# Retention and MLP on one core: folding decay into the query casts, evacuating attention by ACT, and issuing crossbar transposes from SP

## The chip, the cores and the metric

The kernel runs on one core of one Trainium2 chip. The metric is device time in microseconds (us) of one execution; a kernel is executed several times, and medians and ranges are given. Profiles show one execution each, so a profile's span is close to the median but need not equal it.

In the profile, PE is the matmul engine and PEld its weight loads, DVE the vector engine, ACT the scalar engine, POOL the GpSimd engine, and SP the engine that only issues DMAs. A name such as SPq or ACTq means the instruction queue of that engine, when it issues DMAs.

## The reference

Eight batches of eight heads, sequence 576, head dimension 64. Attention is a causal retention: scores are scaled by 1/8 and multiplied by a decay gamma to the power of the distance. The result feeds an MLP whose activation is h * cos(h).

```python
scores = scale * q @ k.T
ret    = scores * where(i >= j, gamma[h] ** (i - j), 0)
x      = (ret @ v)            # reordered to [4608 tokens, 512]
h      = x @ w_in             # 512 -> 2048
out    = (h * cos(h)) @ w_out # 2048 -> 512
```

## The kernel before

The sequence is cut into 40 chunks of 128 positions (the last of each batch has 64). For each chunk the kernel loads K, Q and V in float32, casts them to bf16, transposes K and Q, computes scores inside the chunk, adds the contribution of a running state, and writes the result `XT` for the MLP. The MLP works on nine blocks of 512 tokens: `mlp1` (four matmuls, a cosine on ACT, a product on DVE) sixteen times, then `mlp2` (sixteen matmuls for each of four output tiles, evacuated by ACT into `os`). Attention for a later block is interleaved with the MLP pieces of the current ones.

In this program every engine has its own list of instructions and waits at each until what it needs is ready. A DMA is issued by an instruction in one engine's list, so the issue waits its turn there and holds up whatever follows (a timeline below shows a cosine held up for 3.76 us in this way). The parts that matter:

```python
# decay on the output side: one multiply per chunk on DVE (UP is a table of gamma^i / 8)
def ev_o(g, ob, key):   DVE: XT = ob * UP                 # 128x512
def ev_st(g):           DVE: two copies 64x256, state ST -> SBD
def ev_s(g):            DVE: PT = SC * TRI                # 128x1024
def cast_q(d, engs):    POOL: two plain casts 128x512     # K: a cast; V: a multiply by gamma^-j

# transposes for chunk >= 10, by DMA through the crossbar, in ACT's queue
def move_k(g):          ACT: dma_start_transpose(KT <- NAT)    # waits until POOL has cast
def move_q(d):          ACT: dma_start_transpose(QT <- QNAT)
# (chunks 0..9: transposed by PE, most copied out of PSUM by ACT)

def step(g):            # one unit of attention work
    mm_inter(g); mm_st(g); mm_intra(g); mm_s(g + 1)        # PE
    ev_o(g); ev_st(g); ev_s(g + 1)                         # DVE, back to back

BYPE, LEAD = 10, 2
def T(g):               # called before step(g - 1)
    if g < BYPE: transposes of chunk g by PE
    x = g + LEAD
    if x >= BYPE: move_q(x), move_k(x)
    load_to(g + LEAD + 4); cast_to(g + LEAD + 2)
```

The attention score, state and output matmuls write PSUM; the MLP and the attention outputs share a rotation of five PSUM banks, one or two of them held by `mlp2`. The program lets a bank be written again only after its readers on ACT and DVE are done.

## Time and profile before

| | before |
|---|---|
| median, range (first three executions) | 347.7 us, 345.6 to 349.9 |
| profiled span | 346.2 us |
| PE busy | 89% |
| DVE, ACT, POOL busy | 56%, 41%, 28% |

The first two parts of the profile page of the kernel before: busy time per engine, and the span in 40 slices of 8.7 us (a digit is the busy share in tenths; PEclk is the granted PE clock in tenths; in the DMA row, a digit is the mean busy share of the DMA engines).

```profile
PE 307.4 (89%) x2337; PEld 158.8 (46%) x2374; DVE 194.1 (56%) x335; ACT 141.6 (41%) x233; POOL 96.2 (28%) x138
PE   6489998676779987999999989999998999999997
ACT  6727533435324433433343334443434333444421
PEclk9879999968789999999999999999999999999999
DMA  9999898999944996496747993666742101100012
```

PE looks nearly full, but an average hides stages. In slices 7 to 12 (52 to 104 us) PE is at 6 to 8 tenths, its clock falls, and DMA is saturated until about 95 us. After that PE is near full, and DMA is in most slices not.

To measure stages I use landmarks that every run has: the moments at which ACT begins to evacuate the output tiles `os`. There are 37 of them; the fourth ends block 0, the fifth is the first of block 1. Before, these are at 42.2 us (first), 57.3 (fourth), 107.6 (fifth) and 343.8 (last). Between the fourth and fifth lie all of `mlp1` of block 1 and the first pieces of block 2.

The view of waits of the kernel before (who waited for what: total us, number of times, longest) names the releasers (a selection).

```profile
PEld bk L444 <- DVE xt L399: 9.4, 10, 1.8
PEld bk L466 <- ACT os L481: 9.0, 13, 2.1
PE bk L444 <- DVE gt L454: 8.0, 5, 2.6
PE bk L444 <- DVE xt L399: 7.5, 8, 1.8
ACT cb L451 <- POOL nat L228: 6.0, 2, 3.8
PE bk L466 <- ACT os L481: 4.2, 4, 1.6
```

The fifth line is odd at first sight: a cosine (`cb`) reads nothing that POOL writes. The timeline of ACT between 61 and 67 us shows why it waited. Lines hold start, duration, engine, source line, operation, operands and, in brackets, the idle time before.

```profile
61.96 0.59 ACT L226 ACTIVATE kt<-bk 128x512 bf16<-128x512 bf16 x1
63.21 1.33 ACTq L302 DMA_TRANSPOSE qt<-qnat  x1
64.57 1.69 ACTq L296 DMA_TRANSPOSE kt<-nat  x1
66.30 0.95 ACT L451 ACTIVATE cb<-bk,cpi 128x320 bf16<-128x320 f32 x2 [3.76 <-POOL nat L228]
```

The transpose of Q stands in ACT's queue and waits for POOL's cast, which waits for a load. Then two issues take 1.33 and 1.69 us. Only then can ACT compute the cosines; DVE's products wait for these, and PE for DVE's (`gt`, the third line of the waits).

### The profile page before, as it was taken

The numbers are of one execution on the slowest core, as the hardware profiler recorded it, in microseconds if no ns is written. First come the engines' busy times: TensorE is split into PE (matmuls) and PEld (weight loads), VectorE is DVE, ScalarE is ACT, GpSimd is POOL, SyncE is SP. The second block draws the span as 40 slices with busy tenths as digits, with TensorE's granted clock in tenths as the row PEclk, the third lists the DMA queues.
The fourth block names the chain that finished last, engine by engine and source line by source line (L and its number), as shares of the span: only waits on it lengthen the run. The fifth ranks groups of instructions, "written<-read, shape, count | busy, mean of one in ns | idle before, by whom it ended". The sixth has DMA issues, their size and how long they took to land.

```text
span 346.2 us, 6065 instructions
## 1 busy us (share of the span) xinstructions
PE 307.4 (89%) x2337; PEld 158.8 (46%) x2374; DVE 194.1 (56%) x335; ACT 141.6 (41%) x233; POOL 96.2 (28%) x138
## 2 busy tenths in 40 slices
PE   6489998676779987999999989999998999999997
PEld 2355454444645434444454444444444444444444
DVE  3677524566764766556675756565764666433300
ACT  6727533435324433433343334443434333444421
POOL 3560357446413341331331531422330000000000
PEclk9879999968789999999999999999999999999999
DMA  9999898999944996496747993666742101100012
GB/s 187 234 186 192 197 234 218 213 242 243 214 87 84 213 242 122 103 212 152 148 104 114 249 211 97 157 148 169 136 118 66 47 31 56 38 32 30 30 61 93
DMA packets 133117, 49.43 MB, mean 143 GB/s; under 512 B 105312, under 2 KB 128608, under 8 KB 133088
## 3 DMA queue, kind: packets, MB, share of 16 engines
q1 hardware_dynamic: 99152, 37.76, 49.1%
q10 hardware_dynamic: 29184, 7.08, 13.1%
q0 software_dynamic: 4752, 4.19, 7.8%
q8 instruction: 19, 0.31, 0.4%
q14 instruction: 10, 0.08, 0.1%
HBM read 36.70 MB, written 9.44 MB: 133 GB/s over the span
## 4 chain that ended last, share of the span: by engine, by line
PE 70%; ACT 6%; issue 6%; DVE 4%; POOL 4%; ACTq 3%; DMA 3%; SPq 3%; DVEq 0%; POOLq 0%
PE bk L444 33%; PE bk L466 29%; ACT cb L451 3%; ACTq L296 3%; SPq L198 2%; PE sc L320 2%; POOL nat L238 2%; DVE gt L454 2%; PE st L346 2%; DMA stg<-in_v_dram 2%; PE bk L387 2%; POOL qnat L228 2%; DVE xt L399 1%; PE bk L372 1%; DMA qstg<-in_q_dram 1%
## 5 line engine op out<-in xcount | busy, mean ns | idle before, releaser
L451 ACT ACTIVATE cb<-bk,cpi 128x512 bf16<-128x512 f32 (+3 forms) x164 | 102.6, 635 | 159.4 <-PE bk L444 119.7
L444 PE MATMUL bk<-xt,win 128*128 128x512 bf16 (+3 forms) x634 | 147.3, 363 | 21.0 <-DVE gt L454 8.0
L454 DVE TENSOR_TENSOR gt<-bk,cb 128x512 bf16<-128x512 f32 (+3 forms) x164 | 100.7, 624 | 108.8 <-ACT cb L451 87.0
L466 PE MATMUL bk<-wout,gt 128*128 128x512 bf16 (+1 forms) x578 | 142.7, 374 | 5.5 <-ACT os L481 4.2
L444 PEld LDWEIGHTS bk<-xt,win 128*128 128x128 bf16 x656 | 62.5, 101 | 80.7 <-DVE xt L399 9.4
L466 PEld LDWEIGHTS bk<-wout,gt 128*128 128x128 bf16 x592 | 56.1, 98 | 71.0 <-ACT os L481 9.0
L228 POOL CAST nat<-stg 128x512 bf16<-128x512 f32 (+1 forms) x36 | 21.9, 609 | 127.7 <-PE st L346 80.2
L331 DVE TENSOR_TENSOR pt<-sc,tri 128x1024 bf16<-128x1024 f32 (+1 forms) x40 | 44.6, 1114 | 7.7 <-PE sc L320 6.7
L238 POOL TENSOR_TENSOR nat<-stg,wv 128x512 bf16<-128x512 f32 (+1 forms) x40 | 41.6, 1041 | 18.8 <-DMA stg<-in_v_dram 18.7
L481 ACT ACTIVATE os<-bk 128x512 f32<-128x512 f32 (+1 forms) x37 | 21.7, 585 | 30.2 <-PE bk L466 25.5
L399 DVE TENSOR_TENSOR xt<-bk,up 128x512 bf16<-128x512 f32 (+1 forms) x40 | 26.7, 669 | 11.8 <-PE bk L387 10.9
L228 POOL CAST qnat<-qstg 128x512 bf16<-128x512 f32 (+1 forms) x44 | 25.8, 613 | 13.9 <-DMA qstg<-in_q_dram 13.9
L359 DVE CAST sbd<-st 64x256 bf16<-64x256 f32 x64 | 26.5, 414 | 1.0
L320 PE MATMUL sc<-qt,kt 64*128 64x128 bf16 (+1 forms) x320 | 15.9, 222 | 1.4 <-DVE qt L228 1.2
L387 PE MATMUL bk<-pt,nat 128*64 128x128 bf16 (+1 forms) x320 | 15.8, 223 | 0.5 <-DVE pt L331 0.5
L372 PEld LDWEIGHTS bk<-qt,sbd 128*128 128x128 bf16 x128 | 9.7, 102 | 7.4 <-ACT os L481 1.5
L372 PE MATMUL bk<-qt,sbd 128*128 128x128 bf16 (+1 forms) x128 | 12.0, 218 | 1.0 <-ACT os L481 1.0
L320 PEld LDWEIGHTS sc<-qt,kt 64*128 64x128 bf16 (+1 forms) x320 | 9.3, 100 | 6.1 <-issue 1.7
L387 PEld LDWEIGHTS bk<-pt,nat 128*64 128x64 bf16 (+1 forms) x320 | 10.4, 114 | 1.6 <-DVE pt L331 1.1
L346 PE MATMUL st<-nat 128*64 128x64 bf16 x256 | 10.4, 205 | 0.2 <-POOL nat L238 0.2
L346 PEld LDWEIGHTS st<-nat 128*64 128x64 bf16 x256 | 6.8, 114 | 5.9 <-issue 3.5
L226 ACT ACTIVATE kt<-bk 128x512 bf16<-128x512 bf16 (+1 forms) x10 | 5.5, 550 | 4.6 <-PE bk L266 4.6
(35 smaller groups left out, 46.5 us busy)
## 6 DMA issues: line engine op xcount, KB each, us to landing
out_dram<-os SPq DMA_DIRECT2D x35, 256.0 KB, 2.3
stg<-in_k_dram SPq DMA_DIRECT2D x32, 256.0 KB, 5.0
qstg<-in_q_dram SPq DMA_DIRECT2D x16, 512.0 KB, 5.8
stg<-in_v_dram SPq DMA_DIRECT2D x32, 256.0 KB, 5.8
wout<-in_moe_w_out_dram POOLq DMA_DIRECT2D x4, 512.0 KB, 13.8
win<-in_moe_w_in_dram POOLq DMA_DIRECT2D x3, 512.0 KB, 6.0
stg<-in_k_dram SPq DMA_DIRECT2D x8, 128.0 KB, 3.7
qstg<-in_q_dram SPq DMA_DIRECT2D x8, 128.0 KB, 3.4
```

Source lines behind the costliest of these rows:

```text
L228: self.P.add(eng, lambda e: e.tensor_copy(dst, src), r=r, w=w)
L238: self.P.add(eng, lambda e: e.tensor_tensor(ap(self.NAT[na], 2 * DM, 0, n, DM, [D, H], [1, D]), ap(self.STG[st], 2 * DM, 0, n, DM, [D, H], ...
L320: inst = e.matmul(ap(self.SC, 1024, 0, n, hp * 512 + c * 128, [1, n]), ap(kt, DM, 64 * hp, 64, c * 128, [1, n]), self.queries(g, 64 * hp, ...
L331: self.P.add("dve", lambda e: e.tensor_tensor(ap(pt, 1024, 0, n, 0, [128, 8], [h, 2], [1, h]), ap(self.SC, 1024, 0, n, 0, [128, 8], [h, 2] ...
L359: self.P.add("dve", lambda e, hp=hp: e.tensor_copy(ap(self.SBD[g % self.NSB], 512, 64 * hp, 64, 64 * hp, [128, 4], [1, 64]), ap(self.ST, 5 ...
L372: inst = e.matmul(ap(ob, 512, 0, 128, c * 128, [1, n]), ap(sbd, 512, 0, 128, c * 128, [1, 128]), self.queries(g, 0, 128, c), start=(c == 0 ...
L387: inst = e.matmul(ap(ob, 512, 64 * hp, 64, c * 128, [1, n]), ap(na, 2 * DM, 0, n, DM + (2 * c + hp) * D, [1, D]), ap(pt, 1024, 0, n, hp * ...
L399: self.P.add("dve", lambda e: e.tensor_tensor(ap(self.XT, 4 * TOK, 0, 128, b * S + CH * r, [TOK, 4], [1, 2], [2, h]), ap(ob, 512, 0, 128, ...
L444: inst = e.matmul(ap(ps, 512, 0, 128, 0, [1, n]), ap(self.WIN, 4 * DFF, 0, 128, c * DFF + 128 * f, [1, 128]), ap(self.XT, 4 * TOK, 0, 128, ...
L451: self.P.add("act", lambda e: e.activation(ap(cb, TB, 0, 128, 0, [1, n]), ap(ps, 512, 0, 128, 0, [1, n]), AF.Sin, bias=self.CPI.ap(), scal ...
L454: self.P.add("dve", lambda e: e.tensor_tensor(ap(gt, NF * TB, 0, 128, f * TB + lo - TB * j, [1, n]), ap(ps, 512, 0, 128, 0, [1, n]), ap(cb ...
L466: return e.matmul(ap(ps, 512, 0, 128, 0, [1, cn]), ap(gt, NF * TB, 0, 128, f * TB + 128 * t, [1, 128]), ap(self.WOUT, NF * DM, 0, 128, f * ...
```

## The change

Its intent was to relieve DVE and ACT at once. The decay and the scale are multiplied into Q when it is cast, so the output evacuation becomes a plain copy and can go to ACT, as can the state. The 48 transposes go to SP, which computes nothing, ahead of the next loads, and three chunks early instead of two. The score and state evacuations become separate units, spread between MLP pieces. The early transposes' copies go to DVE (those of K for the first four chunks stay on ACT), and the order of the first four chunks changes. The core of the diff:

```diff
-    self.P.add("act", lambda e: e.dma_start_transpose(   # move_k, move_q
+    self.P.add("sp", lambda e: e.dma_start_transpose(
-    cast_q: copy
+    cast_q: tensor_tensor(..., WT[gamma^i / 8] broadcast, mult)     # POOL (chunks 0..3: DVE and POOL)
-    ev_o: dve tensor_tensor(XT, ob, UP, mult)
+    ev_o: self.copy("act", XT, ob)
-    ev_st: dve tensor_copy x2
+    ev_st: self.copy("act", ...) x2
     def step(self, g):
         ...
         self.ev_o(g, ob, key)
-        self.ev_st(g)
-        if g + 1 < len(CHUNKS):
-            self.ev_s(g + 1)
-        BYPE, LEAD = 10, 2
+        BYPE, LEAD = 10, 3
-                    self.step_tq(dbl(g))
-                self.step_tk(g)
+                    self.step_tq(dbl(g), "dve")
+                self.step_tk(g, "dve")
                 out += [lambda g=g: T(g + 1), lambda g=g: self.step(g)]
+                if g + 1 < NC:
+                    out.append(lambda g=g: self.ev_s(g + 1))
+                out.append(lambda g=g: self.ev_st(g))
[... decay tables UP (ACT, 8 instructions) replaced by a 128x88 table; the head reordered: the first weights
 gated on chunk 1's V instead of chunk 2's K, 8 instead of 4 pieces of mlp1 in halves of 256 columns ...]
```

More of the change, by code (lines that the diff above doesn't have):

```diff
@@ L124, in __init__ @@
         self.OS = [sb(f"os{i}", [128, DM], F32) for i in range(self.NOS)]
-        self.UP = sb("up", [128, 4 * S], F32)
-        self.WV = sb("wv", [128, 40], F32)
+        self.WT = sb("wt", [128, 88], F32)
         self.IDN = sb("idn", [128, 128], BF16)
@@ L130, in __init__ @@
         self.DUM = sb("dum", [128, 512], BF16)
-        self.IG = sb("ig", [128, S], F32)
-        self.IV = sb("iv", [128, 40], F32)
-        self.LV = sb("lv", [128, 40], F32)
-        self.LU = sb("lu", [128, 4], F32)
+        self.IV = sb("iv", [128, 88], F32)
+        self.LV = sb("lv", [128, 88], F32)
         self.CLN = sb("cln", [128, 1], F32)
@@ L154, in constants @@
         lng = [math.log(1.0 - 2.0 ** (-5.0 - h)) for h in range(H)]
-        P.add("pool", lambda e: e.iota(ap(self.IG, S, 0, 128, 0, [1, 512]), [[128, 4], [1, 2], [2, 64]], base=0,
-                                       channel_multiplier=0, allow_small_or_imprecise_dtypes=True), w=["ig0"])
-        P.add("pool", lambda e: e.iota(self.IV.ap(), [[128, 5], [0, 8]], base=0, channel_multiplier=1,
-                                       allow_small_or_imprecise_dtypes=True), w=["iv"])
+        P.add("pool", lambda e: e.iota(ap(self.IV, 88, 0, 128, 0, [1, 40]), [[128, 5], [0, 8]], base=0,
+                                       channel_multiplier=1, allow_small_or_imprecise_dtypes=True), w=["iv0"])
@@ L159, in constants @@
+        P.add("pool", lambda e: e.iota(ap(self.IV, 88, 0, 128, 40, [1, 48]), [[256, 3], [1, 2], [0, 8]], base=0,
+                                       channel_multiplier=2, allow_small_or_imprecise_dtypes=True), w=["iv1"])
         P.add("dve", lambda e: e.memset(self.ONE.ap(), 1.0), w=["one"])
         P.add("dve", lambda e: e.memset(self.DUM.ap(), 0.0), w=["dum"])
+        for h in range(H):
+            P.add("dve", lambda e, h=h: e.memset(ap(self.LV, 88, 0, 128, h, [8, 5]), -lng[h]), w=[("lv", h)])
+            P.add("dve", lambda e, h=h: e.memset(ap(self.LV, 88, 0, 128, 40 + h, [8, 6]), lng[h]), w=[("lv", h + 8)])
@@ L161, in constants @@
         P.add("dve", lambda e: e.memset(self.CLN.ap(), math.log(1.0 / 8.0)), w=["cln"])
-        for h in range(H):
-            P.add("dve", lambda e, h=h: e.memset(ap(self.LU, 4, 64 * (h % 2), 64, h // 2, [1, 1]), lng[h]),
-                  w=[("lu", h)])
-        for h in range(H):
-            P.add("dve", lambda e, h=h: e.memset(ap(self.LV, 40, 0, 128, h, [8, 5]), -lng[h]), w=[("lv", h)])
+        P.add("dve", lambda e: e.memset(self.CPI.ap(), math.pi / 2), w=["cpi"])
         P.add("dve", lambda e: e.tensor_tensor(self.LV.ap(), self.IV.ap(), self.LV.ap(), ALU.mult),
-              r=["iv"] + [("lv", h) for h in range(H)], w=["lvx"])
@@ L169, in constants @@
-        P.add("dve", lambda e: e.memset(self.CPI.ap(), math.pi / 2), w=["cpi"])
+              r=["iv0", "iv1"] + [("lv", h) for h in range(16)], w=["lvx"])
         for i in range(self.NSB):
             P.add("dve", lambda e, i=i: e.memset(self.SBD[i].ap(), 0.0), w=[("sbd", i)])
-        self.decay(0, 256, "ig0")
-        P.add("act", lambda e: e.activation(self.WV.ap(), self.LV.ap(), AF.Exp), r=["lvx"], w=["wv"])
+        P.add("act", lambda e: e.activation(ap(self.WT, 88, 0, 128, 0, [1, 40]), ap(self.LV, 88, 0, 128, 0, [1, 40]),
+                                            AF.Exp), r=["lvx"], w=["wv"])
@@ L174, in constants @@
+        P.add("act", lambda e: e.activation(ap(self.WT, 88, 0, 128, 40, [1, 48]), ap(self.LV, 88, 0, 128, 40, [1, 48]),
+                                            AF.Exp, bias=self.CLN.ap()), r=["lvx", "cln"], w=["wq"])
         P.add("pool", lambda e: e.affine_select(self.IDN.ap(), self.ONE.ap(), pattern=[[1, 128]],
@@ L179, in constants @@
                                                 channel_multiplier=-1), r=["one"], w=["tri"])
-        P.add("pool", lambda e: e.iota(ap(self.IG, S, 0, 128, 512, [1, 64]), [[1, 2], [2, 32]], base=512,
-                                       channel_multiplier=0, allow_small_or_imprecise_dtypes=True), w=["ig1"])
-    def decay(self, lo, hi, *keys):
-        for c in range(4):
-            self.P.add("act", lambda e, c=c: e.activation(
-                ap(self.UP, 4 * S, 0, 128, c * S + lo, [1, hi - lo]), ap(self.IG, S, 0, 128, lo, [1, hi - lo]), AF.Exp,
-                bias=self.CLN.ap(), scale=ap(self.LU, 4, 0, 128, c, [1, 1])),
-                r=list(keys) + ["cln", ("lu", 2 * c), ("lu", 2 * c + 1)], w=[("up", lo, c)])
+        self.sin_table()
     def sin_table(self):
@@ L240, in cast_v @@
             ap(self.STG[st], 2 * DM, 0, n, DM, [D, H], [1, D]),
-            ap(self.WV, 40, 0, n, 8 * r, [1, H], [0, D]), ALU.mult),
+            ap(self.WT, 88, 0, n, 8 * r, [1, H], [0, D]), ALU.mult),
             r=[("stg", st, 1), "wv"], w=[("nat", na, 1)])
@@ L246, in cast_q @@
         for x, eng in enumerate(engs):
-            self.copy(eng, ap(self.QNAT[k], 2 * DM, 0, n, x * DM, [D, H], [1, D]),
-                      ap(self.QSTG[k], 2 * DM, 0, n, x * D, [2 * D, H], [1, D]), [("qstg", k)], [("qnat", k, x)])
+            self.P.add(eng, lambda e, x=x: e.tensor_tensor(
+                ap(self.QNAT[k], 2 * DM, 0, n, x * DM, [D, H], [1, D]),
+                ap(self.QSTG[k], 2 * DM, 0, n, x * D, [2 * D, H], [1, D]),
+                ap(self.WT, 88, 0, n, 40 + 16 * (d % 3) + 8 * x, [1, H], [0, D]), ALU.mult),
+                r=[("qstg", k), "wq"], w=[("qnat", k, x)])
     def bank(self, hold=False):
@@ L301, in move_q @@
         n, k, t = (128, 128, 32)[d % 3], d % self.NQ, d % self.NQT
-        self.P.add("act", lambda e: e.dma_start_transpose(
+        self.P.add("sp", lambda e: e.dma_start_transpose(
             ap(self.QT[t], 2 * DM, 0, 128, 0, [128, 8], [1, n]), ap(self.QNAT[k], 2 * DM, 0, n, 0, [1, 2 * DM])),
@@ L358, in ev_st @@
         for hp in range(2):
-            self.P.add("dve", lambda e, hp=hp: e.tensor_copy(
-                ap(self.SBD[g % self.NSB], 512, 64 * hp, 64, 64 * hp, [128, 4], [1, 64]),
-                ap(self.ST, 512, 64 * hp, 64, 0, [64, 4], [1, 64])),
-                r=["st"], w=[("sbd", g % self.NSB, hp)])
+            self.copy("act", ap(self.SBD[g % self.NSB], 512, 64 * hp, 64, 64 * hp, [128, 4], [1, 64]),
+                      ap(self.ST, 512, 64 * hp, 64, 0, [64, 4], [1, 64]), ["st"], [("sbd", g % self.NSB, hp)])
     def mm_inter(self, g, ob, key):
@@ L398, in ev_o @@
         h = n // 2
-        self.P.add("dve", lambda e: e.tensor_tensor(
-            ap(self.XT, 4 * TOK, 0, 128, b * S + CH * r, [TOK, 4], [1, 2], [2, h]),
-            ap(ob, 512, 0, 128, 0, [128, 4], [h, 2], [1, h]),
-            ap(self.UP, 4 * S, 0, 128, CH * r, [S, 4], [h, 2], [1, h]), ALU.mult),
-            r=[key] + [("up", 0 if r < 2 else 256, c) for c in range(4)], w=[("xt", g)])
+        self.copy("act", ap(self.XT, 4 * TOK, 0, 128, b * S + CH * r, [TOK, 4], [1, 2], [2, h]),
+                  ap(ob, 512, 0, 128, 0, [128, 4], [h, 2], [1, h]), [key], [("xt", g)])
     def step_s(self, g):
@@ L562, in warm @@
             self.P.add("pe", mm, r=["one", "dum"], w=[("bk", 0)])
-        def heads(g):
-            self.cast_k(g, "act")
-            if pair(g):
-                self.cast_q(dbl(g), ("act", "dve"))
-            self.cast_v(g, "pool")
-            self.step_tk(g)
-            if pair(g):
-                self.step_tq(dbl(g), "dve")
+        two = ("dve", "pool")
         load_to(4)
         warm(8)
-        heads(0)
+        self.cast_k(0, "act")
+        self.cast_q(0, two)
+        self.cast_v(0, "pool")
+        self.step_tk(0)
+        self.step_tq(0, "dve")
         warm(2)
@@ L578, in schedule @@
         self.step_st(0)
-        warm(2)
         self.cast_k(1, "act")
@@ L582, in schedule @@
         self.step_tk(1)
-        self.decay(256, S, "ig0", "ig1")
-        self.sin_table()
+        warm(2)
         self.step_o(0)
@@ L587, in schedule @@
         self.step_st(1)
+        self.load_win(0, 1, [("stg", 1, 1)])
+        self.load_win(1, 1)
         warm(2)
-        self.load_win(0, 1, [("stg", 2, 0)])
-        self.load_win(1, 1)
         self.cast_k(2, "act")
-        self.cast_v(2, "pool")
         self.step_tk(2)
         self.step_o(1)
-        self.cast_q(1, ("act", "dve"))
+        self.cast_q(1, two)
+        self.load_win(2, 2)
         self.step_tq(1, "dve")
         self.step_s(2)
+        self.mlp1(0, 256, 0)
+        self.mlp1(0, 256, 1)
+        self.cast_v(2, "pool")
+        self.load_win(4, 2)
         self.step_st(2)
-        self.load_win(2, 2)
         self.cast_k(3, "act")
+        self.step_tk(3)
+        self.step_o(2)
+        self.mlp1(0, 256, 2)
+        self.mlp1(0, 256, 3)
+        self.step_s(3)
         self.cast_v(3, "pool")
-        self.load_win(4, 2)
         self.load_win(6, 2)
@@ L607, in schedule @@
         load_to(9, [("wout", 2)])
-        cast_to(6)
-        self.step_tk(3)
-        self.step_o(2)
-        self.mlp1(0, 256, 0)
-        self.step_s(3)
-        self.mlp1(0, 256, 1)
+        cast_to(7)
         self.step_st(3)
-        self.mlp1(0, 256, 2)
+        for f in (4, 5):
+            self.mlp1(0, 256, f)
         self.step_o(3)
-        self.mlp1(0, 256, 3)
-        for f in range(4):
+        for f in (6, 7):
+            self.mlp1(0, 256, f)
+        for f in range(8):
             self.mlp1(256, 512, f)
-        for f in range(4, 16):
+        for f in range(8, 16):
             self.mlp1(0, 512, f)
```

## The prediction

> **What bounds the kernel now.** The page gives a span of 346.2 us with PE busy 89%, but the loss is uneven. A back-to-back 512-column matmul takes 0.216 us, so the 1,152 MLP matmuls need 249 us. A chunk's attention block takes PE 1.1 us (126.41 to 127.53 in the timeline), so 40 chunks need about 42 us; with the early PE transposes, PE's floor is an estimated 295 us. Where the other 51 us go (windows and timeline):
> - 0 to 21 us: PE has almost nothing. Around 11.7 to 14.5 us it waits for ACT, which computes the second half of the decay table (2.28 us) and loads the Sin table (1.28 us) before it casts K of chunk 2.
> - 55 to 100 us: PE busy 13.3 of 20 and 18.7 of 25 us, granted clock 0.88 and 0.77. I count 22 us of full-clock PE work between 57 and 98 us, so some 18 us are lost. Two causes: DMA is saturated (share 1.15 to 1.21), and crossbar transposes sit in ACT's queue, so ACT blocks until POOL has cast the chunk (idle 3.8 and 2.2 us "until POOL nat") and then spends 1.28 us issuing each. PE waits for the cosines in return, and its clock drops.
> - 98 us to the end: estimated PE floor 236 us plus 2.5 us of tail, 248 taken; some 10 us lost to "PE waits for ACT os" (9.0 us of weight loads, 13 times) and for DVE xt (6.0), at full clock.
>
> **What the change does.**
> - ACT loses 48 transpose issues x 1.28 = 61 us and 5 us of decay; gains 40 output evacuations (estimate 0.59 us, as its like-sized copies) and 64 state evacuations (about 0.37 us): +47 us. What matters more: ACT no longer waits for casts.
> - DVE loses 26.7 + 26.5 us; takes the ten head chunks' transposed copies, about +7 us. Its burst per chunk shrinks from 2.8 us to 1.2 us, and the pieces are spread between MLP units.
> - POOL: q casts become multiplies, 1.04 instead of 0.61 us (it already does this multiply for v): about +19 us, to 33%. In the DMA-bound stretch an estimated 2.9 us per chunk, against about 3.75 us of DMA per chunk, so still off the path, with less room.
> - SP: +61 us of issue. It waits for casts ahead of later loads, but two chunks of loads are in flight then. DMA work is unchanged. The Trainium skill, "DMA: Bandwidth & Descriptors", Issuing engines are not separate DMA queues, says a second issuing engine only saves sequencer time; ACT's 1.28 us per issue and the saturated DMA share agree.
>
> **Gain.** Head: about 3 us on PE, but chunk 4's loads still wait for w_out (released at 35.8 us), so PE's transpose of chunk 4 cannot move up much: 1.5 us. 57 to 98 us: DMA delivers chunk 15 at about 81 us (estimate), so the stretch could end near 84; PE, ACT and DVE would all be near 80% full, so I take 88: 8.5 us more. Afterwards: 5 of 10 us. Sum 15 to 16 us: **332 us**, range 323 to 341. Faster by over 2%: 0.82; within: 0.14; slower: 0.04.
>
> **What would show it.** "ACT cb waits for POOL" gone; "PE(ld) waits for ACT os" under 4 us; ACT busy about 183 us, DVE about 148, POOL about 115; PE clock in 55 to 90 us above 0.9; steady MLP stage (first out-store of block 1) beginning about 10 us earlier; first MLP matmul near 18 us.
>
> **What would make it wrong.** SP stuck behind a transpose that waits for a cast, starving DMA; one ring for loads and transposes delaying transposes more than three chunks cover; POOL becoming the pace in 40 to 90 us; the head's gain lost in waiting for chunk 4.

## More of the kernel before

The next view is the busy time of the engines in two stretches of the kernel before, the middle one and the steady one; the columns are window, length, then busy us with the count of instructions for PE, PEld, DVE, ACT and POOL, then granted clock, DMA share, GB/s.

```profile
57.40:107.60 50.20, 37.48 (x387) 24.57 (x390) 31.26 (x63) 18.56 (x41) 23.77 (x34) 0.83 1.03 188
107.60:344.00 236.40, 223.37 (x1567) 109.39 (x1594) 131.89 (x203) 92.24 (x141) 47.50 (x66) 1.00 0.54 119
```

In the middle stretch PE is idle for 12.7 of 50.2 us and the rest runs at a mean clock of 0.83. In the steady stretch it is idle for 13 of 236.4 us, at full clock.

In the steady stretch there is no waiting for casts, but the issue itself remains. This is ACT, and the PE matmul that waited for it, at 122 to 126 us.

```profile
122.28 1.19 ACTq L302 DMA_TRANSPOSE qt<-qnat  x1
123.51 1.27 ACTq L296 DMA_TRANSPOSE kt<-nat  x1
124.89 0.60 ACT L481 ACTIVATE os<-bk 128x512 f32<-128x512 f32 x1 [1.92 <-PE bk L444]
...
125.54 0.82 PE L466 MATMUL bk<-wout,gt 128*128 128x512 bf16 x3 [1.57 <-ACT os L481]
```

The page puts ACT's 1.92 us of idle time down to a PE matmul, because issue instructions are not counted as busy and leave no releaser. One has to see the two ACTq lines above it.

## The result, and the profile after

| | before | after |
|---|---|---|
| median, range (4 executions each) | 346.67 us, 344.94 to 349.94 | 327.67 us, 326.06 to 328.30 |
| ratio, 95% interval | | 0.9434 (0.9352 to 0.9517) |
| profiled span | 346.2 us | 324.3 us |

The result is correct and 5.7% faster. Ratios here and below are the mean time of one kernel's runs over that of the other's in the same rounds, so not quite the ratio of the medians. Executions over 1.5% slower than the fastest of the same kernel are left out of the means.

The same parts of the page, after:

```profile
PE 302.4 (93%) x2354; PEld 156.1 (48%) x2390; DVE 150.0 (46%) x245; ACT 180.8 (56%) x322; POOL 117.1 (36%) x139
PE   5669999897899999999999999999999999999996
ACT  5568612877754656555556556455556555444511
PEclk9598999999999999999999999999999999999999
DMA  8999999999999999996499739485611000100012
```

DVE's share fell and ACT's rose, as intended. The clock's dip in the middle is gone; the one in the head stays. DMA is saturated for longer in a shorter span.

The stretches between the same landmarks after the change (58.1 and 94.2 are its fourth and fifth output tiles, 321.9 the last):

```profile
58.10:94.20 36.10, 31.03 (x362) 20.55 (x364) 22.47 (x47) 26.83 (x59) 21.38 (x26) 1.00 1.12 211
94.20:322.00 227.80, 222.70 (x1565) 108.26 (x1592) 99.16 (x134) 122.92 (x207) 63.62 (x72) 1.00 0.59 128
```

| stretch | before | after | difference |
|---|---|---|---|
| start to block 0's last output tile | 57.3 | 58.1 | +0.7 |
| to block 1's first output tile | 50.3 | 36.1 | -14.2 |
| to the last output tile | 236.2 | 227.7 | -8.5 |
| last tile to the end | 2.4 | 2.4 | 0 |

So the head gained nothing, and the time came from the middle stretch and from the steady one.

The waits after, those that answer to the lines shown before:

```profile
PEld bk L450 <- ACT os L465: 10.3, 25, 1.2
PE bk L450 <- ACT os L465: 1.9, 5, 0.7
PE sc L312 <- DMA kt<-nat: 0.4, 1, 0.4
```

No line "ACT cb waits for POOL" is left, and none in which PE waits for `xt`. PE's own waits for `os` fell from 4.2 to 1.9 us and the longest weight-load wait from 2.1 to 1.2 us. The sum of the weight-load waits did not fall (9.0 to 10.3 us), but PE's own waits are what counts, and they are 1.9 us.

SP's queue after the change, between 66 and 72 us, shows transposes and loads taking turns:

```profile
66.86 1.26 SPq L288 DMA_TRANSPOSE kt<-nat  x1
68.17 0.59 SPq L187 DMA_DIRECT2D stg<-in_k_dram  x1
68.80 0.57 SPq L187 DMA_DIRECT2D stg<-in_v_dram  x1
69.42 1.15 SPq L468 DMA_DIRECT2D out_dram<-os  x1
70.62 1.22 SPq L288 DMA_TRANSPOSE kt<-nat  x1
```

An issue costs as much on SP as it did on ACT, 1.2 to 1.3 us; but nobody stands behind it except other DMAs.

### The profile page after: what moved, and what is told of

It reads as the page before. It is cut to its first block, busy times and chain, and to the rows that moved or that the text cites. A ratio compares the mean times of both kernels' runs of the same rounds, so it can differ in the third digit from the quotient of the medians.

```text
span 324.3 us, 6144 instructions
## 1 busy us (share of the span) xinstructions
PE 302.4 (93%) x2354; PEld 156.1 (48%) x2390; DVE 150.0 (46%) x245; ACT 180.8 (56%) x322; POOL 117.1 (36%) x139
## 4 chain that ended last, share of the span: by engine, by line
PE 87%; ACT 5%; DMA 3%; issue 3%; DVE 1%; POOL 0%; SPq 0%; DVEq 0%; ACTq 0%; POOLq 0%
PE bk L450 38%; PE bk L428 36%; PE sc L312 4%; PE bk L377 3%; PE st L338 2%; PE bk L362 2%; ACT cb L435 2%; DMA qstg<-in_q_dram 1%; DMA kt<-nat 1%; ACT sbd L215 1%; ACT os L465 1%; PE bk L258 1%; PE bk L277 1%; ACT nat L215 1%; DVE gt L438 0%
## 5 line engine op out<-in xcount | busy, mean ns | idle before, releaser
L438 DVE TENSOR_TENSOR gt<-bk,cb 128x512 bf16<-128x512 f32 (+3 forms) x168 | 102.1, 613 | 134.9 <-ACT cb L435 128.2
L435 ACT ACTIVATE cb<-bk,cpi 128x512 bf16<-128x512 f32 (+3 forms) x168 | 104.0, 627 | 84.9 <-PE bk L428 82.6
L428 PE MATMUL bk<-xt,win 128*128 128x512 bf16 (+3 forms) x651 | 142.9, 350 | 3.7 <-issue 1.9
L450 PEld LDWEIGHTS bk<-wout,gt 128*128 128x128 bf16 x592 | 54.7, 98 | 68.6 <-ACT os L465 10.3
L236 POOL TENSOR_TENSOR qnat<-qstg,wt 128x512 bf16<-128x512 f32 (+1 forms) x46 | 47.4, 1049 | 18.1 <-DMA qstg<-in_q_dram 11.2
L227 POOL TENSOR_TENSOR nat<-stg,wt 128x512 bf16<-128x512 f32 (+1 forms) x40 | 41.6, 1040 | 8.9 <-DMA stg<-in_v_dram 5.1
L215 ACT ACTIVATE xt<-bk 128x512 bf16<-128x512 f32 (+1 forms) x40 | 27.5, 688 | 21.8 <-PE bk L377 21.5
L215 ACT ACTIVATE sbd<-st 64x256 bf16<-64x256 f32 x64 | 23.8, 372 | 5.6 <-PE st L338 4.6
L362 PEld LDWEIGHTS bk<-qt,sbd 128*128 128x128 bf16 x128 | 9.0, 98 | 8.7 <-ACT cb L435 2.5
L258 PE MATMUL bk<-idn,nat 128*128 128x128 bf16 (+1 forms) x40 | 4.1, 232 | 4.6 <-ACT nat L215 3.7
(33 smaller groups left out, 41.6 us busy)
```

The source lines that it names most:

```text
L215: self.P.add(eng, lambda e: e.activation(dst, src, AF.Copy), r=r, w=w)
L227: self.P.add(eng, lambda e: e.tensor_tensor(ap(self.NAT[na], 2 * DM, 0, n, DM, [D, H], [1, D]), ap(self.STG[st], 2 * DM, 0, n, DM, [D, H], ...
L236: self.P.add(eng, lambda e, x=x: e.tensor_tensor(ap(self.QNAT[k], 2 * DM, 0, n, x * DM, [D, H], [1, D]), ap(self.QSTG[k], 2 * DM, 0, n, x ...
L362: inst = e.matmul(ap(ob, 512, 0, 128, c * 128, [1, n]), ap(sbd, 512, 0, 128, c * 128, [1, 128]), self.queries(g, 0, 128, c), start=(c == 0 ...
L428: inst = e.matmul(ap(ps, 512, 0, 128, 0, [1, n]), ap(self.WIN, 4 * DFF, 0, 128, c * DFF + 128 * f, [1, 128]), ap(self.XT, 4 * TOK, 0, 128, ...
L435: self.P.add("act", lambda e: e.activation(ap(cb, TB, 0, 128, 0, [1, n]), ap(ps, 512, 0, 128, 0, [1, n]), AF.Sin, bias=self.CPI.ap(), scal ...
```

## The experiments

Several things changed at once, and two theories could explain the gain. Theory A: ACT stood in its queue waiting for casts and spent 1.28 us on every issue, and this held up the cosines and output tiles on which PE depends. Rival B: DVE's bursts of evacuations held PSUM banks, and moving them to ACT was what helped. Twelve kernels were run. Three groups of four ran on three different chips, each beside the kernel before on the same chip, so I compare across groups by ratio. The intervals of the ratios are about 0.006 to 0.01 wide on each side, mostly from the kernel before's own spread; kernels of one group can be compared by medians more closely, to about 1 us.

### The unedited yardstick, e0_changed_again

> The changed kernel unedited, as the yardstick for the runs beside it on this chip. Both theories: ratio to before 0.935 to 0.952, 326 to 329 us.

Measured: 328.20 us (328.06 to 328.45), ratio 0.9434 (0.9378 to 0.9489). The result repeats.

### Only the queue: e1_sp_only

```diff
 # kernel before, move_k and move_q
-    self.P.add("act", lambda e: e.dma_start_transpose(
+    self.P.add("sp", lambda e: e.dma_start_transpose(
```

> The kernel before with one thing changed: the 48 crossbar transposes are issued from SP instead of ACT (still two chunks early; decay, evacuations and schedule as before). Theory A (ACT standing in its queue for casts and spending 1.28 us per issue was the main cost): two thirds or more of the gain comes with this alone, 331 to 337 us; the waits of ACT cosines for POOL are gone and the stage from 57 to 98 us ends near 88. Rival B (DVE's bursts of 2.8 us per chunk, which hold PSUM banks, were the main cost): at most a quarter of the gain, 342 to 347 us, and PE still waits for DVE xt.

Measured: 333.82 us (332.37 to 335.42), ratio 0.9595 (0.9530 to 0.9661). One word in two places gives 4.05 of the 5.66 per cent, 72% of the gain, as theory A expected. Its stretches:

```profile
59.40:99.30 39.90, 32.62 (x389) 22.34 (x390) 31.13 (x63) 19.04 (x41) 20.55 (x29) 0.96 1.05 217
99.30:330.00 230.70, 226.38 (x1596) 109.41 (x1594) 132.52 (x203) 93.39 (x141) 50.33 (x70) 1.00 0.57 123
```

The middle stretch fell from 50.2 to 39.9 us and the clock in it rose from 0.83 to 0.96, with DVE exactly as busy as before (31.1 against 31.3 us). The steady stretch fell by 5.7 us, to 230.7 (to 230.4 between the exact landmarks). The waits of cosines for POOL are gone. PE's waits for DVE `xt` remain, 5.6 us in nine waits, so what rival B points at is real, but smaller.

### The queue undone: e2_act_issue

```diff
 # kernel changed, move_k and move_q
-    self.P.add("sp", lambda e: e.dma_start_transpose(
+    self.P.add("act", lambda e: e.dma_start_transpose(
```

> The changed kernel with only the 48 transposes put back on ACT (three chunks early, everything else as changed). Theory A: most of the gain is lost, 338 us or more, because ACT now has evacuations and issues: busy 181 plus 61 us of issue, with stalls of PE behind both. Rival B: still 330 us or less.

Measured: 338.74 us (337.95 to 339.45), ratio 0.9728 (0.9658 to 0.9798): 10.5 us slower than the unedited kernel beside it, just above the value that theory A gave as its least. The timeline of ACT in this run, where block 0 ends, and the next matmul of PE:

```profile
61.20 1.33 ACTq L294 DMA_TRANSPOSE qt<-qnat  x1
62.57 1.64 ACTq L288 DMA_TRANSPOSE kt<-nat  x1
64.25 0.74 ACT L215 ACTIVATE xt<-bk 128x512 bf16<-128x512 f32 x1 [6.92 <-POOL nat L227]
64.85 0.58 ACT L465 ACTIVATE os<-bk 128x512 f32<-128x512 f32 x1
...
65.49 0.72 PE L428 MATMUL bk<-xt,win 128*128 128x320 bf16 x2 [4.20 <-ACT os L465]
```

ACT idles for 6.92 us (3.9 us for POOL's cast, then 3.0 us for two issues), while an attention output and an output tile stand behind them. PE had finished its matmuls for both by 61.3 us, and then idled 4.20 us for the bank. The same stall as before the change now delays evacuations too. Adding the queue alone gains 13 us and removing it alone loses 10.5 us; the parts are not additive, and I have not settled how they overlap.

### Evacuations back on DVE: e4_dve_evac

```diff
 # kernel changed, ev_st and ev_o
-    self.copy("act", ap(self.SBD...   self.copy("act", ap(self.XT...
+    self.copy("dve", ap(self.SBD...   self.copy("dve", ap(self.XT...
```

> The changed kernel with the output and state evacuations put back on DVE as plain copies (transposes on SP, decay folded). DVE busy then about 200 us, ACT about 130. Theory A: little is lost, 327 to 332 us. Rival B: more than half of the gain is lost, 336 us or more, and PE waits for DVE again in the steady stage.

Measured: 328.39 us (328.04 to 329.51), ratio 0.9444 (0.9386 to 0.9502), the same as the yardstick's 328.20. Rival B falls in the form in which I stated it: once the transposes are off ACT, which engine evacuates makes no difference to the total. DVE was busy for 194.1 us in the first 300 us, as much as in the whole of the kernel before. The stretches differ, though. The middle one took 39.8 us, against 35.6 in the yardstick, at a clock of 0.91 instead of 1.00, and three waits of PE for DVE's copies of the state appeared, which the yardstick's profile does not have:

```profile
PE bk L362 <- DVE sbd L217: 3.3, 3, 1.9
```

The other kernels with transposes on SP and all evacuations on DVE also needed 39.9 us there (e1_sp_only, e9_sp_and_split), and four others with evacuations on ACT, different in lead or head, from 35.6 to 36.1 (the profile after, e3, e6, e8). Those in which PE waited longer for a transposed K needed 37 to 41.5 (e5, e10, e11, e12). So in the middle stretch the move to ACT was worth up to 4 us in these single profiles, and rival B has a part there. In the total it does not show: in this profile the head was 2.9 us shorter (granted clock of the first 38 us 0.96, against 0.73) and the steady stretch 1.0 us shorter (226.7 against 227.7). Why these nearly cancel, I have not shown.

### Two chunks early instead of three: e3_lead2

```diff
-        BYPE, LEAD = 10, 3
+        BYPE, LEAD = 10, 2
```

> The changed kernel with the transposes (and loads and casts) two chunks early instead of three. Theory A (the third chunk only covers the delay of a transpose that now stands behind loads in SP's queue): 1 to 4 us slower than the changed kernel, with PE waiting for kt or qt between 60 and 86 us. Rival C (SP would starve the loads or the lead is what made the gain): 6 us slower or more. No difference would mean that the lead is worth nothing.

Measured: 326.90 us (325.26 to 328.60), ratio 0.9413 (0.9337 to 0.9490). No slower. Both expectations miss; the run says what its last sentence says, that the third chunk of lead is worth nothing here. The view of waits of this run has a single line in which PE waits for a DMA of `kt`, 0.4 us in one wait, just as in the profile after, and none for `qt`.

### The burst restored: e5_unsplit

```diff
 # kernel changed: evacuations back in step(), no units of their own
         self.ev_o(g, ob, key)
+        self.ev_st(g)
+        if g + 1 < len(CHUNKS):
+            self.ev_s(g + 1)
 ...
-                if g + 1 < NC:
-                    out.append(lambda g=g: self.ev_s(g + 1))
-                out.append(lambda g=g: self.ev_st(g))
```

> The changed kernel with the evacuations of scores and state back inside the attention step, instead of being separate units between MLP pieces. If the prediction's reading is right that spreading them matters because bursts hold PSUM banks: 2 to 5 us slower. If with ACT and DVE sharing the work the bursts are already short enough: within 1 us.

Measured: 330.92 us (330.29 to 332.05), ratio 0.9516 (0.9457 to 0.9575). It is 3 to 4 us slower than the three other kernels of its group, which all ran at 326.9 to 328.1. The waits of PE name the banks:

```profile
PE sc L312 <- DMA kt<-nat: 5.1, 2, 3.7
PE bk L431 <- ACT xt L215: 3.8, 7, 0.7
PE bk L431 <- DVE gt L441: 2.0, 4, 0.7
```

(This edit shifts the source lines by three: L431 is `mlp1`'s matmul.) The second and third lines are PE waiting for a bank that ACT or DVE had not yet released. From block 1's first tile to the last it took 230.5 us, against 227.7 in the profile after. The first line is another matter: the edit also halves the number of attention units, so transposes and steps fall between other MLP pieces, and two waits for a transposed K appeared. This run therefore does not measure the split alone in the middle stretch; the steady stretch does not have that wait.

### Queue and split without the rest: e9_sp_and_split

```diff
 # kernel before: transposes on "sp" (as e1_sp_only), and
         self.ev_o(g, ob, key)
-        self.ev_st(g)
-        if g + 1 < len(CHUNKS):
-            self.ev_s(g + 1)
 ...
+                if g + 1 < NC:
+                    out.append(lambda g=g: self.ev_s(g + 1))
+                out.append(lambda g=g: self.ev_st(g))
```

> The kernel before with two things changed: transposes issued from SP, and the score and state evacuations as separate units between MLP pieces (no folding, all evacuations on DVE, two chunks early, old head). If the queue and the split are the whole gain: 328 to 331 us, that is ratio 0.945 to 0.955. If folding and the moved evacuations carry the other 3 us: 332 to 334 us, as with the queue alone.

Measured: 329.67 us (329.01 to 331.80), ratio 0.9478 (0.9431 to 0.9524). That is 5.2 of the 5.66 per cent, 92% of the gain. Its steady stretch, from block 1's first tile to the last, took 226.7 us, against 230.4 with the queue alone: 3.7 us for the split, roughly what its removal cost in e5_unsplit's steady stretch (2.8 us). By ratio, what is left for folding, the moved evacuations, the third chunk of lead and the new head together is 0.4 per cent, less than the intervals can separate from zero. It need not be zero: two variants of the changed kernel beside this run on the same chip (e10 and e11 below, which also have dummy matmuls) had medians of 327.5 and 327.6 us, 2 us faster, and its middle stretch took 39.9 us against 36.1 in the profile after.

### The old head: e6_head_old_order

```diff
 # kernel changed; the first four chunks in the order of the kernel before, e.g.
-        self.load_win(0, 1, [("stg", 1, 1)])
+        self.load_win(0, 1, [("stg", 2, 0)])
-        for f in range(8):
+        for f in range(4):
             self.mlp1(256, 512, f)
 [... and mlp1 pieces 0 to 3, the casts of chunks 2 and 3, and the weight loads where they were ...]
```

> The changed kernel with the first four chunks scheduled in the old order (four early MLP pieces of 256 columns instead of eight, weights gated on chunk 2's K, casts where they were), decay still folded. The profiles before and after both start the second matmul of block 0 at 38.4 us, so I expect no difference: within 1.5 us. 3 us or more slower would mean that the new head order did gain and the profile of one execution hides it.

Measured: 328.11 us (327.06 to 329.01), ratio 0.9431 (0.9371 to 0.9490). No difference, as expected. The reordered head brings its first MLP matmul forward (18.9 us after, 21.0 before, 22.6 in this run) and gains nothing in the total.

### A faster head, three attempts: e8_mixed_evac, e10_warm_head, e11_warm_k3_early

Could the head be made to count? Three edits of the changed kernel tried.

```diff
 # e8_mixed_evac
-    self.copy("act", ap(self.SBD...  / ap(self.XT...
+    self.copy("dve" if g < 4 else "act", ...
 # e10_warm_head: dummy matmuls in PE's gaps
         self.step_tk(0)
+        warm(6)
         self.step_tq(0, "dve")
 [... also 5 before step_tk(1), 2 more before cast_k(2), 3 before step_s(2), 5 before step_tk(3) ...]
 # e11_warm_k3_early: as e10, and
         self.step_s(2)
+        self.cast_k(3, "act")
         self.mlp1(0, 256, 0)
```

> The changed kernel with outputs and states of the first four chunks evacuated by DVE and the rest by ACT. The run with all evacuations on DVE had its first output ready at 40.8 us against 44.8 beside it, but needed 4 us more between block 0 and block 1. Theory D (the head's time is paid in full, and ACT's queue in the head delays the K casts): 324 us, 3 to 4 us faster than the changed kernel. Rival E (the loads released by w_out set when block 1 can start, so a faster head only waits longer): within 1 us of it.

> The changed kernel with 21 more dummy matmuls put into gaps of PE in the first 22 us, to hold its clock. Across five profiles the time at which block 0's first output is ready varies from 41.6 to 44.8 us with the clock granted in the head, and block 1's first follows 51.3 to 51.8 us later each time. Theory D (the head is paid in full and its spread is the clock): granted clock of the first 38 us above 0.95, first output near 40 us, 323 to 325 us in all. Rival E (the loads set block 1): 327 to 329 us although the head is faster.

> As the run with the warm head, and ACT's cast of chunk 3's K moved ahead of the first two cosine pieces, since its data is there by 16 us and PE waits for it at 20 to 22 us. Theory D: 1 to 1.5 us faster than the warm head alone, 322 to 324 us. Rival E: no difference.

Measured: 327.12 us (326.54 to 330.70), ratio 0.9425; 327.49 us (325.58 to 329.03), ratio 0.9404; 327.63 us (326.14 to 329.04), ratio 0.9409. None differs from the changed kernel's 0.9434 by more than its interval.

e8_mixed_evac did not speed up the head in its profile (first output tile at 43.3 us), so it says nothing about the question. The other two did. With dummy matmuls the granted clock of the first 38 us was 1.00 (0.87 in the profile after, 0.73 in the yardstick's), and the first output tile came at 40.6 and 39.6 us, against 42.3 and 44.8 (the fourth at 57.6 and 56.9, against 58.1 and 60.5). Yet block 1's first tile came at 95.0 and 95.9 us, against 94.2 and 96.1. Theory D, that the head is paid in full, had come from five profiles in which the first tile was at 41.6 us or later; below that, the outcome is the one that rival E expected. The chain of what ended last in e11_warm_k3_early, between 69 and 85 us, shows to whom the time went (start, us, what):

```profile
70.08 1.22 SPq L288
71.34 4.28 DMA stg<-in_k_dram
75.68 0.26 POOL nat L217
75.94 0.31 issue
76.25 2.03 POOL qnat L236 x2
78.34 6.43 DMA kt<-nat
84.82 0.61 PE sc L312 x8
```

A load takes 4.28 us to land, POOL casts K and then both halves of Q (2.03 us), and a transpose takes 6.43 us to land, among loads that saturate DMA; 2.81 us of it is the issue. In this run PE waited for it 1.95 us at 84.8 us, and before that the chain runs through DMA and POOL, not PE. That `w_out` sets when these loads start, as rival E says, was not tested.

### Loads ahead of transposes: e12_loads_first

```diff
             x = g + LEAD
+            load_to(g + LEAD + 4)      # moved up, before move_q / move_k
             if BYPE <= x < NC:
                 ...
-            load_to(g + LEAD + 4)
```

> The changed kernel with SP's queue reordered: the next chunk's loads ahead of the transposes instead of behind them. If the order matters because a transpose then stands behind one more chunk of loads: 1 to 3 us slower. Since two and three chunks early took the same time, I expect no difference, within 1 us.

Measured: 330.74 us (329.86 to 331.90), ratio 0.9506 (0.9458 to 0.9554). Slower by about 3 us than the two other variants of the changed kernel in its group (327.5 and 327.6), and so in the range of the expectation's first sentence, not of its conclusion. The order in SP's queue matters where the distance in chunks does not. In its profile the middle stretch took 37.4 us against 35.6 in the yardstick, with first tiles at the same 44.8 us. In its profile the transposes of Q stood in SP's queue for POOL's casts for 28.8 us in 13 waits, against 9.8 us in 7 in the profile after; I have not shown that these make the difference.

## Why the prediction was right, and where its steps were not

The range held the result (323 to 341; measured 327.7) and the direction was right. Step by step:

- *The transposes in ACT's queue are what costs.* Right, and shown by adding the change of queue alone (72% of the gain) and by removing it alone (10.5 us lost). But I wrote that ACT blocks for a cast and then spends 1.28 us on each issue, and that the wait for casts matters more. The 3.8 and 2.2 us that I quoted for that wait already contain the issues; the wait itself was 0.66 us and nothing. No run separates the two.
- *Middle stretch, 8.5 us.* The direction was right, the size too small: 14.2 us between block 0's last and block 1's first output tile. I had estimated that DMA would allow an end near 84 us and then took 88, to allow for PE, ACT and DVE being near 80% full. The first matmul of 512 columns after that stretch began at 86.4 us (98.5 before), and block 1's first tile followed 7.8 us later instead of 9.1, which I had not counted. The queue alone gave 10.3 of the 14.2 us (e1_sp_only); up to 4 came only with the evacuations on ACT (see e4_dve_evac), a term that my sum did not have. In the profile after, PE's clock stayed at 1.00, against 0.83 before, and PE was busy for 31.0 of 36.1 us. The Trainium skill, "TensorE: Matmul & The Clock Gate", Part 1: The HAM clock gate, says that the clock is halved after a window without enough activity and comes back with sustained work. The traces agree in kind: before the change twelve matmuls of 320 columns at 59.7 us took 1.80 us, 0.15 each, at a granted clock of 1.00, and at 71.5 us, after idle times of PE of 2.6 and 2.1 us, twelve took 3.36 us, 0.28 each, at 0.50. So here a stall cost twice, once as idle time and once as slow matmuls after it; I had named the clock but gave its recovery no size.
- *Steady stretch, 5 of 10 us.* Measured 8.5. The queue gave 5.8 of it (236.2 to 230.4 us, e1_sp_only) and spreading the evacuations 3.7 (to 226.7, e9_sp_and_split); with everything else it is 227.7. The burst argument was right, but in this stretch it was the spreading that mattered and not the engine: e4_dve_evac has all evacuations on DVE and took 226.7 us.
- *Head, 1.5 us.* Wrong in outcome, and my reason is not what the profile after shows. I wrote that the loads released by `w_out` would hold back chunk 4. The result was +0.7 us in the profile, and four head variants made no difference in the total. From 30 to 58.5 us PE waited only 0.2 us there, so no load held it up; in the first 38 us it was busy for 28.9 us (28.0 before) at a lower clock (0.87 against 0.91), which may have taken the saving. With a warmed head PE did wait, 1.1 us for POOL's cast of chunk 5's Q, and e10 and e11 show that a head whose first tile comes 1.7 and 2.7 us earlier is given back before block 1.
- *Busy times.* Estimated 183, 148 and 115 us for ACT, DVE and POOL; measured 180.8, 150.0 and 117.1. One term was off: the output evacuation on ACT took 0.746 us per full chunk, where I had 0.59 from its other copies of 512 elements.
- *Signs.* "ACT waits for POOL" is gone, the clock is above 0.9, block 1's first output tile came 13.5 us earlier (I had said 10), and the first MLP matmul was at 18.9 us. The sign "PE(ld) waits for ACT os under 4 us" failed: 1.9 us for PE, but 10.3 us for weight loads. That was a badly chosen sign: what PE itself waited is what counts.
- *What could have made it wrong.* SP did not starve DMA: its mean share stayed at 1.13 from 40 to 100 us. Sharing a ring with the loads did not slow the transposes as a rule: from issue to landing K's took a median of 3.0 us (at most 5.2), against 3.9 (at most 8.4) in ACT's own queue before. One of 6.43 us, behind POOL's longer casts, did hold PE up for 1.95 us in e11_warm_k3_early, and e5_unsplit has 5.1 us of such waits; in the profile after there are 0.4 us.

No run clearly beat the changed kernel. A kernel with the queue and the split alone comes within 0.4 per cent of it by ratio with far fewer edits. Left open: how the parts overlap (13 us added alone, 10.5 us lost when removed alone), why the up to 4 us gained in the middle stretch by evacuating on ACT do not show in the total, and why the order in SP's queue costs 3 us while a chunk of lead costs none.

## What to carry to other kernels

A DMA issue should not stand in the queue of an engine that computes for the critical one, even if it seems cheap and its data is ready; look for waits whose named releaser has no business with the waiting instruction, and for the issue lines hidden in an engine's idle time. When a change bundles several moves, add each one alone to the old kernel and remove it alone from the new one: here one word in two places and a reordering carried 92% by ratio, and folding, engine, lead and head together were worth about 2 us or less. Compare the stretches too, since two kernels of equal total can differ by 4 us in one of them. Once the first stall is gone, measure where the next limit lies before making earlier stages faster, since a faster head gained nothing here.

## What the Trainium skill lacked or had wrong

- "DMA: Bandwidth & Descriptors", Issuing engines are not separate DMA queues, says that issuing on several engines only saves the sequencer's time, "which is usually small relative to the DMA itself". Here a crossbar transpose took 1.26 us to issue (median on SP, 1.28 on ACT) and 3.0 us from issue to landing for K in the profile after. The section does not say that the choice of engine costs time where that engine also computes: moving 48 issues from ACT to SP was worth 13 us (e1_sp_only).
- "ScalarE: Activation LUTs", What ACT_TABLE_LOAD costs, gives 186 ns + 0.833 N for an ACTIVATE with immediate scale and bias, so an estimated 0.61 us for 512 elements. The copies into contiguous tiles agree (0.597 us for `os`), but the one that writes every second bf16 element of `XT` took 0.746 us. The page's formula has no term for the access pattern; no run here isolated the pattern as the cause.
- "SBUF — State Buffer", SBUF: two separate sides, says that a VectorE instruction with two SBUF inputs and a GpSimd instruction that reads SBUF exclude one another, the later one blocking. In the head after the change one such pair overlapped in the timeline, and POOL's multiply took 1.54 us instead of 1.04:

```profile
6.14 0.69 DVE L236 TENSOR_TENSOR qnat<-qstg,wt 128x512 bf16<-128x512 f32 x1 [3.50 <-ACT kt L215]
6.19 1.54 POOL L236 TENSOR_TENSOR qnat<-qstg,wt 128x512 bf16<-128x512 f32 x1 [4.42 <-ACT kt L215]
```

  That agrees with the page only roughly: blocked until DVE's end at 6.83 us, POOL would have lost 0.64 us, and it lost 0.50 (again 1.54 us in e0, e3 and e8; spans on POOL are rough). PE's transposes of Q wait for it (2.5 us until POOL `qnat`). No experiment here isolated it.
- No page has the time from issue to landing of a crossbar transpose among loads. For K it was 2.4 to 5.2 us (median 3.0) from SP in the profile after, 2.4 to 8.4 us (median 3.9) from ACT before, and 6.43 us at most in e11_warm_k3_early.
